# A fused attention and expert kernel: when the attention stage asks for its loads

## The chip, the cores and the metric

The kernel runs on one core of a Trainium2 chip. The core has a matrix engine (TensorE, PE in the profile; its weight loads are the row PEld), a vector engine (VectorE, DVE), a scalar engine (ScalarE, ACT), a general engine (GpSimd, POOL) and an engine that here only issues transfers (SyncE, SP). Each engine works through its own queue in order; the queues wait for each other through semaphores. Transfers between device memory and the on-chip memory run on 16 DMA engines. They are issued by SP (loads) and by POOL (results, and gathers and scatters by index).

The metric is the device time of the whole program in microseconds, the median of several runs. The kernel before took 645.92 us (three runs, 644.81 to 647.61).

## The reference: what is computed

Two blocks follow each other, on 8 sequences of 576 tokens with 8 heads of 64 values, all in float32.

```python
# attention, with a window of 64 tokens
scores = scale * np.matmul(q, k.transpose(0, 1, 3, 2))
mask = (rel >= 0) & (rel < window)            # rel = query position - key position
attn = softmax(np.where(mask, scores, -1e9))
x = np.matmul(attn, v)                        # then heads side by side: 512 values a token
...
# one expert of 8 for each token
logits = x @ w_gate                           # 512 x 8
local_gate = sigmoid(x @ w_local)
e = argmax(logits) if first token of a sequence or local_gate < 0.5 else e of the token before
p = softmax(logits)
h = np.maximum(x @ w1[e], 0.0)                # 512 x 1024
out = p[e] * (h @ w2[e])                      # 1024 x 512
```

The expert of a token depends on its attention output, so the sorting of tokens by expert (the router) stands between the two blocks.

## The kernel before, in words

**Attention** treats the 4608 tokens as 9 superchunks of 512, and the 8 heads as 4 pairs. A unit is one superchunk and one pair, written (sc, hp); there are 36, in the order (0, 0), (0, 1) and so on to (8, 3). For a unit TensorE multiplies keys with queries (`scores`, line 385), ScalarE takes the exponential (line 416), VectorE applies the mask (line 421; for some units a bias matmul at line 400 does it instead), TensorE multiplies with the values (`values`, line 431), and VectorE takes the reciprocals of the sums into `allr` (line 436) and scales the result into `x` (line 441). Scores run two units ahead of values. So the reciprocals at line 436, one for each unit and in order, are a clock by which units can be followed in the trace.

**What is loaded for a superchunk.** `kq` holds keys and queries, 2 MB, in a tile of the ring `ring` (four buffers of 2 MB, shared with the experts' weights). `va` holds the values, 1.0 MB, or 1.2 MB for the superchunks 4 to 8, which have extra room for gate columns; it has three buffers. From `va`, POOL and ScalarE copy a version shifted by 64 tokens, `vb` (lines 360 to 367). For the superchunks 4 to 8 there is also `vtt`, the turned values, 1 MB and one buffer, from which TensorE computes the gate logits of the values (`gates`, line 317). `gates(sc + 1)` runs in unit (sc, 2), and the shift to `vb` of superchunk sc + 1 begins in unit (sc, 0). At the end of a superchunk POOL writes `x`, 1 MB, to device memory (line 533).

**When it is loaded.** All these loads are issued by SP, in the order of the program. Superchunk 0 is asked for at the start. The loads of superchunk 1 stand behind a small transfer `until` (line 239), which reads one number of the first mask and so can't start before the mask is there; everything after it in SP's queue waits with it. The loads of superchunk 2 stand in the same way behind the reciprocals of unit (0, 0). The rest (sc + 2, for sc from 1 to 6) is placed in units (sc, 0) and (sc, 2): the whole of `va`, then two halves of `kq`, and in (sc, 2) the turned values. These wait for nothing but a free buffer: the buffer of `va` is free when the values of superchunk sc - 1 are done (line 228 in SP's waits), that of the turned values when `gates(sc + 1)` are done (line 223).

**The router** for the first part of the tokens runs beside attention (`rt.first`, in pieces handed out by `step`), mostly on VectorE; its table needs lines 790 to 975. It ends with writing each token's weight `ptw` to device memory (`weigh`, line 893, on SP) and with the table of rows for the first expert blocks.

**The experts** work in blocks of 256 tokens of one expert. A block's rows are gathered by index (POOL, line 1148), turned (line 1181), and multiplied with `w1` (line 1379 for the first blocks) and `w2` (line 1411). The first block is job -1. Its weights are asked for while attention still runs: `w1` in four pieces of 512 KB behind the reciprocals of (6, 3), `w2` likewise behind those of (7, 1), both at line 1167. Later blocks ask for their weights when a buffer of the ring is free.

**Order of work.** In attention the order on PE, ACT and SP is the program's own (`manual_schedule`, line 204). On VectorE and POOL a planner at build time orders the instructions, by its own costs and by when it thinks that their inputs are ready.

Of the kernel before, what the change touches and what calls it, by code (L numbers as in the profile page):

```python
# [8 lines left out]
F32 = mybir.dt.float32  # L9
# [6 lines left out]
ET = mybir.EngineType  # L16
# [3 lines left out]
P = 128  # L20
B, H, S, DH = 8, 8, 576, 64
D = H * DH
E, F = 8, 1024
DK, FK = D // P, F // P
# [19 lines left out]
PARTS = 4  # L44
# [16 lines left out]
SC = 4 * P  # L61
NSC = N // SC
HP = H // 2
# [3 lines left out]
VX = DH + 1  # L67
VW = VX + E + 1
GATED = range(4, NSC)
BIASED = [(4, 3), (5, 1), (5, 3), (6, 0), (6, 1), (6, 2), (6, 3)]  # L70
HALF = 0.8
STEP = 3.5
# [5 lines left out]
def row_of(t):  # L78

    return t + (t >= ZR)  # L80
# [87 lines left out]
def attention(ctx, tc, ring, kq, v3, v4, vt, vh, xs, lt, ok, wg, wg2, ident, rt, ex):  # L168
# [37 lines left out]
    kqs, qts, kts, vts, vas, vbs = {}, {}, {}, {}, {}, {}  # L206

    def width(sc):
        return VW if sc in GATED else VX

    def space(name, sc):
        return kp.tile([P, 4, H, width(sc)], F32, name=name, bufs=2 if name == "vb" else 3)


    vhs = tp.tile([P, HP, SC], F32, name="vtt")[:, :, :WIN]
# [2 lines left out]

    def load(sc, parts):
        for part in parts:  # L220
            if part == "turned":
                vts[sc] = tp.tile([P, HP, SC], F32, name="vtt")
                nc.sync.dma_start(out=vts[sc], in_=vt[GATED.index(sc)])
            elif isinstance(part, tuple):
                if sc not in vas:
                    vas[sc] = space("va", sc)
                src, h = v4[GATED.index(sc)] if sc in GATED else v3[sc], slice(*part)
                nc.sync.dma_start(out=vas[sc][:, :, h], in_=src[:, :, h])
            else:
                if sc not in kqs:  # L230
                    kqs[sc] = ring.tile([P, HP, 2, SC], F32, name="w")
                    kts[sc], qts[sc] = kqs[sc][:, :, 0], kqs[sc][:, :, 1]
                nc.sync.dma_start(out=kqs[sc][:, part], in_=kq[sc, :, part])

    late = cp.tile([1, 4], F32, name="late")

    def until(i, x):

        nc.sync.dma_start(out=late[:, i:i + 1], in_=x)

    pairs = slice(0, HP // 2), slice(HP // 2, HP)
    whole = (0, H)
    load(0, [slice(0, 1), slice(1, 2), (0, H // 2), pairs[1], (H // 2, H)])

    def warm(n):

        r = bank()
        for _ in range(n):
            nc.tensor.transpose(r[:, :P], ident, ident)
# [18 lines left out]
    masks = []  # L268
# [26 lines left out]
    allr = cp.tile([P, NSC, HP, 2, 4], F32, name="allr")  # L295
# [12 lines left out]
    def gates(sc):  # L308
# [115 lines left out]
    def values(sc, hp, p, x, g):  # L424
# [12 lines left out]
        rr = r.rearrange("p j (c o) -> p j c o", o=1)  # L437
        if sc in GATED:
            nc.vector.tensor_tensor(g[:, :, hp].rearrange("p c j e -> p j c e"), o[:, :, :, VX:],
# [1 line left out]
        nc.vector.tensor_tensor(x[:, :, hp].rearrange("p c j d -> p j c d"), o[:, :, :, :DH],  # L441
                                rr.to_broadcast([P, 2, 4, DH]), op=Alu.mult)

    units = [(sc, hp) for sc in range(NSC) for hp in range(HP)]
    ps = {}
    masked = []
    for u in units[:LEAD]:
# [2 lines left out]
    with tc.issue_after(masked[-1].ins):  # L450
        build_mask(1)
    warm(24)
    until(0, masks[0][:1, :1])
    load(1, [pairs[0], whole, pairs[1]])
    moves, gated, turned, old = (), None, None, None
    side = None
# [14 lines left out]
    for i, (sc, hp) in enumerate(units):  # L471
        if hp == 0:
            x, g = wk.tile([P, 4, HP, 2, DH], F32, name="x"), None
            if sc in GATED:
                g = wk.tile([P, 4, HP, 2, E + 1], F32, name="g")

        if 1 < i < len(units) - LEAD:
            ps[units[i + LEAD]] = scores(*units[i + LEAD])
        if hp == (0 if sc else 3) and sc + 1 < NSC:
            moves = shift(sc + 1)  # L480
        for _ in range(2 if sc else 4):
            next(moves, None) if moves else None

        if hp == 3 and sc + 1 in GATED:
            spread(sc + 1, gated)
        elif (sc, hp) == (1, 3):
            gates_ahead()
        elif (sc, hp) == (2, 3):
            back_ahead()
        if hp == 3 and sc not in GATED:  # L490
            turn(sc, x, 0)
            old = x
        elif sc and sc - 1 not in GATED:
            if hp == 0:
                turn(sc - 1, old, 1)
            elif hp == 2:
                logits(sc - 1, turned)

        if side is None and 4 * sc >= C1 and hp >= 2:
            side = rt.first(bank)  # L500
        step(not (hp == 3 and sc + 1 in GATED))
        values(sc, hp, ps.pop((sc, hp)), x, g)
        if i < 2:
            ps[units[i + LEAD]] = scores(*units[i + LEAD])
        if i == 0:
            shift_first(1)
            until(1, allr[:1, 0, 0, 0, :1])
            load(2, [pairs[0], whole, pairs[1]])
            nc.sync.dma_start(out=vhs, in_=vh)
        if i == 2 * HP:  # L510
            with tc.issue_after(masked[-1].ins):
                rt.prepare()
                build_bias()
        if hp == 1 and sc and sc - 1 not in GATED:
            turned = gates(sc - 1)
        if hp == 2 and sc + 1 in GATED:
            gated = gates(sc + 1)
        if 0 < sc < NSC - 2 and hp in (0, 2):
            load(sc + 2, [pairs[1]] if hp else [whole, pairs[0]])
        if hp == 2 and sc + 2 in GATED:  # L520
            load(sc + 2, ["turned"])
        if (sc, hp) == (NSC - 3, 3):
            ex.jobs = [ex.weights({}, -1, ("w1",), lambda: until(2, allr[:1, sc, hp, 0, :1]))]
            if side == ():
                ex.rows(ex.jobs[0], -1)
        step(not (hp == 2 and sc + 1 in GATED))
        if (sc, hp) == (NSC - 2, 1):
            ex.weights(ex.jobs[0], -1, ("w2",), lambda: until(3, allr[:1, sc, hp, 0, :1]))
        if hp == HP - 1:
            if sc in GATED:  # L530
                nc.vector.tensor_reduce(lt[:, 4 * sc:4 * sc + 4, :], g.rearrange("p c h j e -> p c e (h j)"),
                                        axis=AX.X, op=Alu.add)
            nc.gpsimd.dma_start(out=xs[row_of(sc * SC):row_of(sc * SC) + SC, :D].rearrange("(c p) d -> p c d", p=P),
                                in_=x.rearrange("p c h j d -> p c (h j d)"))
# [583 lines left out]
class Experts:  # L1118
# [33 lines left out]
        st["pw"] = [x[:, D:D + 1] for x in st["x"]]  # L1152
        return st

    def weights(self, st, n, names=("w1", "w2"), behind=lambda: None):
        ej, at = (self.tabs["ej1"], -1 - n) if n < 0 else (self.tabs["ej"], n)
        e = self.nc.values_load(ej[0:1, at:at + 1], engines=[ET.SP], min_val=0, max_val=E - 1,
                                skip_runtime_bounds_check_because="a count of experts, at most E - 1")
        behind()
        for name, w, a, b in (("w1", self.w1, DK, F), ("w2", self.w2, FK, D)):  # L1160
            if name not in names:
                continue
            t = self.ring.tile([P, a * b], F32, name="w")
            src = w[bass.ds(e, 1)].rearrange("o p x -> (o p) x")
            m = a * b // (PARTS if n < 0 else 1)
            for c in range(0, a * b, m):
                self.nc.sync.dma_start(out=t[:, c:c + m], in_=src[:, c:c + m])
            st[name] = t.rearrange("p (a b) -> p a b", a=a)
        return st

    def begin(self):
        self.jobs = [self.fetch(-1)]
# [395 lines left out]
```

## Time and profile before

| what | value |
|---|---|
| median of three runs | 645.92 us |
| the profiled execution's own time | 646.97 us |
| its span, first to last instruction | 645.2 us |
| mean granted TensorE clock | 0.997 |
| attention, about 0 to 136 us: TensorE busy | 119.42 of 136.00 us |
| experts, 136 to 632 us: TensorE busy | 493.76 of 496.00 us |
| the tail, 632 to 645.2 us: TensorE busy | 6.33 of 13.20 us |
| DMA in attention: share of the 16 engines, rate | 0.94, 356 GB/s |
| DMA in the experts' stage | 0.65, 237 GB/s |
| reciprocals of (0, 0), (2, 0), (6, 0), (7, 0) | 14.22, 41.94, 104.49, 115.13 us |
| reciprocals of (6, 3), (7, 3), (8, 2), (8, 3) | 111.90, 124.10, 131.62, 133.85 us |
| superchunk 8 asked for: `va`, turned values | 97.00, 108.59 us |
| its `gates` on TensorE, its shift on POOL | 118.54; 111.56 and 112.96 us |
| first matmul of the first expert block (w1, w2) | 133.7, 149.2 us |

All times in the trace count from the first instruction. Slices and windows give an engine's busy time; a matmul's end is modelled, so a busy TensorE need not be at its peak. "A <- B: t, n, m" in a list of waits means that A stood idle for B, t us in total, n times, m at the longest. "Issue" as the releaser means that the profile shows nothing that the engine waited for. A line of a timeline gives the start, the length, the engine, the line of the program, the operation and what it writes and reads.

### The profile page before, as it was taken

How to read it: one execution, taken by the hardware profiler on the slowest of the kernel's cores; microseconds unless marked ns; L12 is line 12 of the kernel's file. 1: busy time of each engine (PE TensorE's matmuls, PEld its weight loads, DVE VectorE, ACT ScalarE, POOL GpSimd, SP SyncE). 2: the span in 40 equal slices, each digit the busy share in tenths (PEclk: the TensorE clock that was granted, in tenths of full speed). 3: DMA queues.
4: the chain of work that ended last, by engine and by line, in shares of the span. 5: the costliest groups of instructions: out<-in, count | busy, mean ns of one | idle time of the engine just before them, and what ended most of it. 6: DMA issues, size and time to landing. Idle time of an engine off the chain costs nothing. (4 is left out here: it accounts for less than half of the span.)

```text
span 645.2 us, 14856 instructions
## 1 busy us (share of the span) xinstructions
PE 619.5 (96%) x6319; PEld 535.8 (83%) x6319; DVE 386.7 (60%) x730; ACT 199.9 (31%) x364; POOL 130.0 (20%) x132
## 2 busy tenths in 40 slices
PE   8889998899999999999999999999999999999995
PEld 7777776785859999978998999887997998899995
DVE  6676588853874865273553683362917752876730
ACT  4766665611473122112120312021211221122120
POOL 5322112320003202111212220221312022101101
PEclk9999999999999999999999999999999999999998
DMA  8999999969736655686957655769768557945501
GB/s 331 416 349 344 379 359 368 344 241 356 210 146 233 242 199 197 209 314 244 398 193 274 229 226 217 259 232 366 258 244 302 186 196 255 354 157 221 216 17 38
DMA packets 29318, 166.43 MB, mean 258 GB/s; under 512 B 8451, under 2 KB 9497, under 8 KB 20026
## 3 DMA queue, kind: packets, MB, share of 16 engines
q1 hardware_dynamic: 20394, 135.54, 57.8%
q0 software_dynamic: 8848, 29.85, 11.9%
q8 instruction: 52, 0.85, 0.5%
q14 instruction: 24, 0.20, 0.1%
HBM read 146.18 MB, written 19.59 MB: 257 GB/s over the span
## 5 line engine op out<-in xcount | busy, mean ns | idle before, releaser
L1361 POOL DMA_INDIRECT out_dram<-y,idx x36 | 41.3, 1148 | 347.3 <-DVE y L1297 169.6
L1240 PE MATMUL hp<-xs,ws 128*128 128x128 f32 x672 | 79.6, 275 | 0.0
L1288 PE MATMUL hp<-ws,hs 128*128 128x256 f32 x336 | 77.6, 380 | 0.0
L1240 PEld LDWEIGHTS hp<-xs,ws 128*128 128x128 f32 x672 | 77.3, 192 | 0.0
L1288 PEld LDWEIGHTS hp<-ws,hs 128*128 128x128 f32 x336 | 63.5, 190 | 9.3 <-issue 0.8
L1379 PE MATMUL hp<-xt,w 128*64 128x64 f32 (+2 forms) x640 | 66.3, 276 | 1.0 <-issue 1.0
L1379 PEld LDWEIGHTS hp<-xt,w 128*128 128x128 f32 (+1 forms) x640 | 61.2, 170 | 5.9 <-issue 2.5
L1297 DVE SCALAR_TENSOR_TENSOR y<-hp,xg,kept 128x256 f32<-128x256 f32 x42 | 19.7, 481 | 71.4 <-issue 47.0
L1251 DVE TENSOR_TENSOR h<-hp,keep 128x512 f32<-128x512 f32 x42 | 28.6, 690 | 53.0 <-PE hp L1240 53.0
L1148 POOL DMA_INDIRECT xg<-xs,gx x40 | 48.2, 1205 | 44.3 <-issue 37.6
L1411 PE MATMUL yp<-w,h 128*128 128x512 f32 x128 | 56.6, 593 | 0.0
L1240 PEld LDWEIGHTS hp<-xt,w 128*128 128x128 f32 x448 | 53.2, 192 | 2.7 <-issue 1.3
L1240 PE MATMUL hp<-xt,w 128*128 128x128 f32 x448 | 54.7, 275 | 0.0
L1288 PE MATMUL hp<-w,h 128*128 128x256 f32 x224 | 53.6, 382 | 0.0
L431 PE MATMUL xo<-vb,p 128*64 128x74 f32 (+1 forms) x576 | 44.2, 228 | 6.8 <-issue 3.7
L416 ACT ACTIVATE p<-sp 128x512 f32<-128x512 f32 x72 | 39.2, 596 | 37.1 <-PE sp L385 33.9
L385 PEld LDWEIGHTS sp<-w 64*64 64x64 f32 x1296 | 37.9, 134 | 13.1 <-issue 9.7
L421 DVE TENSOR_TENSOR p<-p,mask 128x1024 f32<-128x1024 f32 x29 | 36.5, 1258 | 19.2 <-ACT p L416 18.9
L431 PEld LDWEIGHTS xo<-vb,p 128*64 128x64 f32 x576 | 38.4, 137 | 10.0 <-issue 5.2
L385 PE MATMUL sp<-w 64*64 64x128 f32 (+1 forms) x1296 | 43.3, 265 | 3.3 <-issue 2.4
L1288 PEld LDWEIGHTS hp<-w,h 128*128 128x128 f32 x224 | 41.3, 190 | 5.6 <-issue 0.4
L431 PE MATMUL xo<-va,p 128*64 128x74 f32 (+1 forms) x576 | 44.5, 228 | 1.5 <-issue 1.5
(280 smaller groups left out, 934.0 us busy)
## 6 DMA issues: line engine op xcount, KB each, us to landing
w<-in_w_dram SPq DMA_DIRECT2D x42, 2048.0 KB, 8.7
w<-in_kq_dram SPq DMA_DIRECT2D x17, 1024.0 KB, 10.2
w<-in_w_dram SPq DMA_DIRECT2D x24, 512.0 KB, 10.0
xs<-x POOLq DMA_DIRECT2D x9, 1024.0 KB
va<-in_v_dram SPq DMA_DIRECT2D x5, 1184.0 KB
vtt<-in_vt_dram SPq DMA_DIRECT2D x5, 1024.0 KB
va<-in_v_dram SPq DMA_DIRECT2D x3, 1040.0 KB, 10.2
va<-in_v_dram SPq DMA_DIRECT2D x2, 520.0 KB, 7.0
```

Of the source, the lines that this page charges most:

```text
L385: nc.tensor.matmul(sp[j][c * WIN:(c + 1) * WIN, a:b], lhsT=kt[h, hp, block * WIN:(block + 1) * WIN], rhs=qt[h, hp, a:b], start=not biased, ...
L416: nc.scalar.activation(p[:, j], sp[j], Act.Exp, scale=DH ** -0.5)
L421: masked.append(nc.vector.tensor_tensor(p, p, m.to_broadcast([P, 2, SC]), op=Alu.mult))
L431: nc.tensor.matmul(xo[par * WIN:(par + 1) * WIN, j, s * VW:s * VW + n], lhsT=p[:, j, b * WIN:(b + 1) * WIN], rhs=w[:, s, 2 * hp + j, :n], ...
L1148: self.nc.gpsimd.indirect_dma_start(out=x, out_offset=None, in_=self.xs[:rows, :], in_offset=bass.IndirectOffsetOnAxis(ap=gx[:, s:s + 1], ...
L1240: nc.tensor.matmul(out[:, m, :], lhsT=a[:, kk, m * P:(m + 1) * P], rhs=b[:, kk, :], start=start and m + kk == 0, stop=stop and (m, kk) == ...
L1251: nc.vector.tensor_tensor(o, x, y, op=add)
L1288: nc.tensor.matmul(out, lhsT=a[:, m, :], rhs=b[:, m, :], start=start and m == 0, stop=stop and m == FK // 2 - 1, skip_group_check=True)
L1297: nc.vector.scalar_tensor_tensor(y[i][:, j * w:(j + 1) * w], x, pw[i], y2, Alu.mult, Alu.add)
L1361: self.nc.gpsimd.indirect_dma_start(out=self.out[:, :], out_offset=bass.IndirectOffsetOnAxis(ap=st["idx"][:, s:s + 1], axis=0), in_=y, in_ ...
L1379: nc.tensor.matmul(hp[a, i, :], lhsT=st["w1"][:, kk, m * P:(m + 1) * P][:, a], rhs=st["xt"][:, kk, :n], start=(kk == 0), stop=(kk == DK - 1))
L1411: nc.tensor.matmul(yp, lhsT=st["h"][:, m, i * P:(i + 1) * P], rhs=st["w2"][:, m, :], start=(m == 0), stop=(m == FK - 1))
```

## The change

The loads of the superchunks 2 to 8 are cut into four shares, one for each unit (sc, hp) of the superchunk two before. Each share stands in SP's queue behind `until` on that unit's reciprocals. The shares for hp = 0 and 1 hold half of `va` (two of its four chunks of 128 tokens) and one pair's part of `kq` (512 KB); those for hp = 2 and 3 hold half of the turned values (512 KB, superchunks 4 to 8 only) and one pair's part of `kq`. The first block's `w1` goes out in four pieces behind the units of superchunk 7, its `w2` in four behind those of superchunk 8, the last one without a wait. The number of the first block's expert is read by SP in unit (7, 0) instead of (6, 3). The loads of superchunks 0 and 1 stay. The loading of later blocks' weights is rewritten through the new function `piece` and issues what it did.

```diff
+UNITS = [(sc, hp) for sc in range(NSC) for hp in range(HP)]
+TURNED = "turned0", "turned1"
...
         for part in parts:
-            if part == "turned":
-                vts[sc] = tp.tile([P, HP, SC], F32, name="vtt")
-                nc.sync.dma_start(out=vts[sc], in_=vt[GATED.index(sc)])
+            if part in TURNED:
+                if sc not in vts:
+                    vts[sc] = tp.tile([P, HP, SC], F32, name="vtt")
+                h = pairs[TURNED.index(part)]
+                nc.sync.dma_start(out=vts[sc][:, h], in_=vt[GATED.index(sc), :, h])
+            elif isinstance(part, int):
+                if sc not in vas:
+                    vas[sc] = space("va", sc)
+                src, c = v4[GATED.index(sc)] if sc in GATED else v3[sc], slice(part, part + 2)
+                nc.sync.dma_start(out=vas[sc][:, c], in_=src[:, c])
...
-    late = cp.tile([1, 4], F32, name="late")
+    late = cp.tile([1, len(UNITS) + 1], F32, name="late")
...
+    def behind(sc, hp):
+        until(allr[:1, sc, hp, 0, :1])
...
         if i == 0:
             shift_first(1)
-            until(1, allr[:1, 0, 0, 0, :1])
-            load(2, [pairs[0], whole, pairs[1]])
-            nc.sync.dma_start(out=vhs, in_=vh)
...
-        if 0 < sc < NSC - 2 and hp in (0, 2):
-            load(sc + 2, [pairs[1]] if hp else [whole, pairs[0]])
-        if hp == 2 and sc + 2 in GATED:
-            load(sc + 2, ["turned"])
-        if (sc, hp) == (NSC - 3, 3):
-            ex.jobs = [ex.weights({}, -1, ("w1",), lambda: until(2, allr[:1, sc, hp, 0, :1]))]
-            if side == ():
-                ex.rows(ex.jobs[0], -1)
+        if sc < NSC - 2:
+            behind(sc, hp)
+            load(sc + 2, [*([2 * hp] if hp < 2 else TURNED[hp - 2:hp - 1] if sc + 2 in GATED else []), slice(hp, hp + 1)])
+        if i == 0:
+            nc.sync.dma_start(out=vhs, in_=vh)
+        if sc == NSC - 2:
+            behind(sc, hp)
+            if hp == 0:
+                ex.jobs = [ex.weights({}, -1, ())]
+                if side == ():
+                    ex.rows(ex.jobs[0], -1)
+            ex.piece(ex.jobs[0], "w1", hp)
         step(not (hp == 2 and sc + 1 in GATED))
-        if (sc, hp) == (NSC - 2, 1):
-            ex.weights(ex.jobs[0], -1, ("w2",), lambda: until(3, allr[:1, sc, hp, 0, :1]))
+        if sc == NSC - 1:
+            if hp < HP - 1:
+                behind(sc, hp)
+            ex.piece(ex.jobs[0], "w2", hp)
...
+    def piece(self, st, name, i):
+
+        a, b = (DK, F) if name == "w1" else (FK, D)
+        if name not in st:
+            st[name] = self.ring.tile([P, a * b], F32, name="w").rearrange("p (a b) -> p a b", a=a)
+        m = a * b // st["parts"]
+        src = (self.w1 if name == "w1" else self.w2)[bass.ds(st["e"], 1)].rearrange("o p x -> (o p) x")
+        self.nc.sync.dma_start(out=st[name].rearrange("p a b -> p (a b)")[:, i * m:(i + 1) * m],
+                               in_=src[:, i * m:(i + 1) * m])
```

More of the change, by code (lines that the diff above doesn't have):

```diff
@@ L233, in load, with until @@
                 nc.sync.dma_start(out=kqs[sc][:, part], in_=kq[sc, :, part])
-    late = cp.tile([1, 4], F32, name="late")
-    def until(i, x):
+    late = cp.tile([1, len(UNITS) + 1], F32, name="late")
+    def until(x):
+        i = next(held)
         nc.sync.dma_start(out=late[:, i:i + 1], in_=x)
+    def behind(sc, hp):
+        until(allr[:1, sc, hp, 0, :1])
+    held = iter(range(len(UNITS) + 1))
     pairs = slice(0, HP // 2), slice(HP // 2, HP)
@@ L442, in values @@
                                 rr.to_broadcast([P, 2, 4, DH]), op=Alu.mult)
-    units = [(sc, hp) for sc in range(NSC) for hp in range(HP)]
+    units = UNITS
     ps = {}
@@ L452, in attention @@
     warm(24)
-    until(0, masks[0][:1, :1])
+    until(masks[0][:1, :1])
     load(1, [pairs[0], whole, pairs[1]])
@@ L1153, in rows, with weights @@
         return st
-    def weights(self, st, n, names=("w1", "w2"), behind=lambda: None):
+    def weights(self, st, n, names=("w1", "w2")):
         ej, at = (self.tabs["ej1"], -1 - n) if n < 0 else (self.tabs["ej"], n)
[L1157 to L1168, printed above, removed]
-        return st
+        st["e"] = self.nc.values_load(ej[0:1, at:at + 1], engines=[ET.SP], min_val=0, max_val=E - 1,
+                                      skip_runtime_bounds_check_because="a count of experts, at most E - 1")
+        st["parts"] = PARTS if n < 0 else 1
+        for name in names:
+            for i in range(st["parts"]):
+                self.piece(st, name, i)
+        return st
+    def piece(self, st, name, i):
[6 more added lines that the diff above has]
+                               in_=src[:, i * m:(i + 1) * m])
     def begin(self):
```

## The prediction

> **What bounds the kernel now.** I read the page first: the span is TensorE's, 96% busy, and the chain that ended last shows only the tail, so time can only be won or lost where TensorE stands idle, or is made to.
>
> ```profile
> PE 619.5 (96%) x6319; PEld 535.8 (83%) x6319; DVE 386.7 (60%) x730; ACT 199.9 (31%) x364; POOL 130.0 (20%) x132
> ...
> q8 instruction: 52, 0.85, 0.5%
> ```
>
> (Queue q8: packets, MB, share.) The waits of TensorE say where. Read the first column as who waited, the right side as total, times, longest. Nearly all of it is "issue", time in which the profile shows nothing that was waited for. The rows left out wait for ScalarE (1.5, 0.8 and 0.6 us) or VectorE (0.9), or belong to the expert stage.
>
> ```profile
> PE xo L431 <- issue: 5.2, 6, 1.8
> PE r L249 <- POOL ident masks.py:199: 2.6, 1, 2.6
> PE sp L385 <- issue: 2.4, 4, 1.1
> PE xo L431 <- DVE x L441: 1.6, 2, 1.2
> ...
> PE xo L302 <- issue: 0.5, 1, 0.5
> ```
>
> These 8.1 us (5.2 + 2.4 + 0.5) are eleven gaps, all in attention. TensorE's timeline puts them at 20.48 (0.51), 27.33 (0.42), 33.53 (0.65), 39.51 (1.09), 46.08 (0.24), 51.91 (0.28), 76.00 (0.69), 100.10 (1.02), 106.59 (0.27), 123.25 (1.18) and 129.43 (1.75 us). Cutting the trace into windows from one gap to the next gives the cause away: look at the counts in brackets behind PE and PEld.
>
> ```profile
> 20.48:27.33 6.85, 5.86 (x127) 4.99 (x127) 4.89 (x8) 6.75 (x10) 2.30 (x3) 1.00 1.02 411
> 27.33:33.53 6.20, 5.55 (x129) 4.20 (x129) 3.24 (x5) 3.88 (x7) 1.69 (x2) 1.00 1.02 422
> 33.53:39.51 5.98, 4.89 (x126) 4.29 (x127) 3.31 (x6) 2.80 (x5) 1.91 (x2) 1.00 0.76 280
> 39.51:46.08 6.57, 6.15 (x129) 4.57 (x128) 5.37 (x26) 4.91 (x8) 1.75 (x4) 1.00 1.00 373
> ...
> 123.25:129.43 6.18, 4.42 (x128) 4.03 (x127) 5.32 (x10) 2.59 (x6) 0.81 (x1) 1.00 1.03 388
> ```
>
> Between gaps lie 253 to 258 instructions each time. The instruction queue moved 0.85 MB in 52 packets, 16.3 KB each; TensorE's 12638 instructions divided by 256 are 49. So I read a gap as TensorE waiting for its next block of instructions, which travels on the same DMA engines as the loads. The last two columns are the DMA share and GB/s: with 411 to 422 GB/s moving the engines are full. From 111 to 115 us they moved 250 GB/s, and TensorE worked 4.00 of 4.00 us through 251 instructions.
>
> That DMA is full as a whole matters too: 373 GB/s from 8 to 112 us against the 420 or so of its fullest windows. The queue's own waits show what paces the requests now: free buffers.
>
> ```profile
> SPq L228 <- PE xo L431: 40.7, 6, 13.5
> ...
> SPq L223 <- PE r L317: 30.1, 4, 8.5
> ...
> SPq L239 <- DVE allr L436: 5.7, 2, 5.3
> ```
>
> **The change, part by part.** Durations are of the profiled execution (646.97 us, span 645.2), which is 1.05 us above the median of 645.92; I carry differences over to the median.
>
> *Waits and requests on SP.* Waits by a 4-byte transfer go from 4 to 36 (mask 1, superchunks 0 to 6: 28, superchunk 7: 4, superchunk 8: 3). The three on allr took 0.62 to 0.66 us of the queue, so 32 more are 20.5 us at 0.64. Loads of superchunks 2 to 8 go from 26 to 52 requests of 0.33 to 0.46 us, another 10 us. A unit's share then costs SP about 0.64 + 2 x 0.4 = 1.4 us of the 3.4 us that a unit lasts. Nothing else is in the queue but the routing weights (109.0 us), so this is free while units last over 1.5 us.
>
> *What the new waits hold up.* Each waits for a unit's reciprocals. Behind it stand that unit's loads, and between units (6, 2) and (6, 3) the writes of ptw. Those already stand behind the turned load, issued at 108.59 once gates(7) were done; the new order reaches them at about 109 as well. POOL's queue keeps its order. The expert's number, read now after (7, 0) at 115.13, was computed by 96.3: nobody waits.
>
> *The gaps.* Superchunks 2 and 3 have no turned load, so the new requests of superchunks 0 and 1 (14.22 to 41.94 us by the reciprocals, 13.9 us each) are 3 MB of loads plus 1 MB of results, about 300 GB/s for 420. The gaps at 27.33, 33.53 and 39.51 (2.16 us) should shrink; bounds are 0 and 2.16, and I take 70%, 1.5, by the unhindered block at 111 to 115. From there to 115.13 us a superchunk moves 5.2 MB (kq 2, va 1.2, turned 1, results 1) per 14.6 us either way, 88% of 420 GB/s in decimal bytes; of the gaps at 46.08, 51.91 and 76.00 (1.21 us) I take 40%, 0.5. The two at 100.10 and 106.59 lie where VectorE is late anyway (below): 0. The gap at 20.48 keeps superchunk 1's burst: 0. At the end, w1 and w2 were asked for as 2 MB each at 114.64 and 121.56; now 0.5 MB a unit. Of 1.18 I take 30%, since the last superchunk's loads are still under way, of 1.75 60%: 1.4. Sum 3.4 us, with bounds 0 and 2.16 + 1.21 + 2.93 = 6.3. A loss is not excluded, since gaps move with the blocks' ends.
>
> [...]
>
> *Smaller requests.* The 0.5 MB pieces of w landed in 10.0 us (median), the 2 MB ones in 8.7; 1 MB of kq in 10.2. Size alone shows no cost here; I take 0.
>
> [...] The windows above hold 422 GB/s with requests of 1 to 1.2 MB in flight, and the sum stays with them.
>
> *Requests that come later.* Before, superchunk 8's va and kq went out at 97.00 us, and its turned values at 108.59. The new requests hang on VectorE, which does the router's table work in the middle of (5, 3):
>
> ```profile
> 93.32 0.20 DVE L436 RECIPROCAL allr<-xo 128x8 f32<-128x8 f32 x1
> ...
> 100.55 1.49 DVE L951 TENSOR_TENSOR rowh<-io,lo 128x1280 bf16<-128x1280 f32 x1
> 101.95 0.20 DVE L436 RECIPROCAL allr<-xo 128x8 f32<-128x8 f32 x1
> ...
> 111.90 0.20 DVE L436 RECIPROCAL allr<-xo 128x8 f32<-128x8 f32 x1
> ```
>
> So from 94 to 102 us nothing is asked for, and the queue runs dry. Then within 102 to 108 come 1 MB for superchunk 7, 1 MB of results and 3.2 MB for superchunk 8: 5.2 MB x 2.62 us (at 400 GB/s) from 103.6 is 117.2; ptw's small packets (the 112 to 114 window moved only 262 GB/s) put it near 120. Behind that comes the second half of superchunk 8's turned values, released at 111.90, issued after ptw near 113.6, landing at about 121.4. The matmuls of gates(8) run at 118.54, so TensorE stops for 2.9 us. The lower end is 0, if it lands in 3.8 us (the fastest row on the ring's tile); the upper, with the slowest, 14.4, is 114 + 14.4 - 119 = 9.4. I take 0.8, nearer the low end, because all of this moves with the router's place on VectorE, and a late TensorE there meets other waits.
>
> *The last quarter of w1* is released by (7, 3) at 124.10 and issued at about 125.0. The first expert matmul starts at 133.7. At the median of 10.0 it lands at 135.0 and costs about 0.5 us; at 3.8 it costs nothing, at 14.4 it costs 4.9. I take 0.3. w2's last piece goes out at about 132.5 and is needed at 149.2: 0. The halves of va are asked for at least 7 us before their copies (105.59 against 112.96 for superchunk 8), and POOL may be late there: 0.
>
> Sum: -3.4 + 0.8 + 0.3 = -2.3. The profiled execution would have taken 644.7, the median is 643.6 us.
>
> **Rivals.** *All gaps close and nothing is late* (14%): -6.3, 639.6 us. For it: light windows have no gap. Against: DMA stays 88% full in the middle.
>
> *The blocks come no sooner* (15%): mean DMA load is the same, the fetch has its own queue, and the lateness is hidden: 645.6 us. For it: the gaps at 46.08 and 51.91 were small with DMA at full 422 GB/s. Against: 111 to 115.
>
> *Slower: a late turned half* (20%): one mechanism, in superchunk 7, gates(8). With the 11.3 us that 1 MB of kq took to land between 90 and 136 us, the half lands at 114 + 11.3 = 125.3, 6.2 us after its matmuls. With half the gain, 1.7, that is +4.5: 650.4 us. It decides from the point where the lateness is over the gain plus 3.2 us. For it: the dry stretch of 94 to 102 us. Against: the half is 0.5 MB and slips as soon as the router moves.
>
> **How the numbers follow.** The forecast has 51%; its own range is 641 to 645.5, from the gain's bounds. About 3.2 us (0.5%) is what a measurement of this kernel can tell from no change. The forecast's 51% split into 24% beyond that and 27% within; with the first rival faster is 38%, with the second same is 42%, slower 20%. The range goes from 639.6 (all gaps closed) to 649.0, which leaves out the worse half of the slower rival.
>
> **What would show it.** Right: the issue gaps every 256 instructions after 24 us are under 0.4 us, DMA share in 24 to 40 us falls below 0.9, SP waits mostly on allr. Wrong: gaps of the same size; TensorE idle before L317 or the first L1379 on a load; VectorE's router work in another place.

## The result, and the profile after

The kernel with the change takes 650.55 us (median of 20 runs, 645.01 to 654.49), the kernel before 646.20 us (20 runs, 644.65 to 650.37) on the same chip. The ratio is 1.006, with a 95% interval of 1.0036 to 1.0084: slower by 0.6%, where I had forecast 0.4% faster. The value lies beyond the top of my range (649.0) and beside the price of my own slower rival (650.4). The profiled execution of the changed kernel took 652.41 us, span 650.7; that of the kernel before 646.97, span 645.2. The profiles are compared with each other below, so there are 5.4 us to explain in them, 1.1 us more than between the medians (4.35).

The page of the kernel after, the same two lines as shown before:

```profile
PE 623.3 (96%) x6319; PEld 537.1 (83%) x6319; DVE 387.7 (60%) x730; ACT 199.8 (31%) x364; POOL 131.3 (20%) x132
...
q8 instruction: 52, 0.85, 0.5%
```

TensorE's work is the same 6319 matmuls and the same 52 packets of instructions, but it is busy for 3.8 us more, and 1.7 us more of the span is idle. The mean granted clock is 0.987 for 0.997, and the same matmuls take longer: those from `vb` into `xo` 234 ns on average for 228. I had not looked for that.

The waits of TensorE in the kernel after (total, times, longest):

```profile
PE r L331 <- DMA vtt<-in_vt_dram: 4.1, 1, 4.1
PE xo L445 <- issue: 2.7, 2, 2.3
PE r L263 <- POOL ident masks.py:199: 2.6, 1, 2.6
PE xo L445 <- DVE x L455: 2.3, 2, 1.9
...
PE sp L399 <- ACT vb L381: 1.2, 1, 1.2
PE sp L399 <- issue: 0.8, 2, 0.4
...
PE xo L316 <- issue: 0.3, 1, 0.3
```

The issue waits fell from 8.1 to 3.8 us (2.7 + 0.8 + 0.3), and one of those left, 2.35 us at 57.76, is new. At the top stands a wait that the kernel before did not have: 4.1 us of `gates` (L331) for the turned values.

SP's timeline around that wait shows how it comes about (start, length, engine, line, what is written and read):

```profile
94.35 0.59 SPq L249 DMA_DIRECT2D late<-allr  x1
95.03 0.33 SPq L227 DMA_DIRECT2D vtt<-in_vt_dram  x1
95.42 0.45 SPq L242 DMA_DIRECT2D w<-in_kq_dram  x1
102.99 0.58 SPq L249 DMA_DIRECT2D late<-allr  x1
...
106.28 0.33 SPq L232 DMA_DIRECT2D va<-in_v_dram  x1
106.66 0.77 SPq L242 DMA_DIRECT2D w<-in_kq_dram  x1
107.53 0.59 SPq L249 DMA_DIRECT2D late<-allr  x1
108.16 0.39 SPq L232 DMA_DIRECT2D va<-in_v_dram  x1
108.60 0.53 SPq L242 DMA_DIRECT2D w<-in_kq_dram  x1
109.56 0.59 SPq L249 DMA_DIRECT2D late<-allr  x1
110.46 0.33 SPq L227 DMA_DIRECT2D vtt<-in_vt_dram  x1
111.05 0.82 SPq L242 DMA_DIRECT2D w<-in_kq_dram  x1
114.91 3.85 SPq L910 DMA_DIRECT2D xs<-ptw  x2
118.86 0.59 SPq L249 DMA_DIRECT2D late<-allr  x1
119.49 0.39 SPq L227 DMA_DIRECT2D vtt<-in_vt_dram  x1
```

Two things are to be read here. First, nothing is asked for from 95.9 to 103.0 us: `until` waits for the reciprocals of (5, 3), and these stand on VectorE behind the router's table and come at 102.76. Second, SP is ready for the writes of `ptw` at 111.87 and issues them at 114.91. SP's waits name what it stood for:

```profile
SPq L249 <- DVE allr L450: 28.4, 16, 4.5
SPq L249 <- DVE g L453: 24.1, 7, 7.3
...
SPq L910 <- DMA va<-in_v_dram: 3.0, 1, 3.0
```

`ptw` has nothing to do with `va`. In this trace SP's 169 transfers name eight completion semaphores (the marks by which a landing is told) in turn, and of the 161 after the first eight none goes out before the one eight places ahead of it has landed; six go out within 0.02 us of that landing. Count back in the timeline: eight requests before `ptw` stands the `va` half of 106.28. It lands at 114.89, and `ptw` goes out at 114.91. Before the change eight requests were some 8 MB; now every third is a 4-byte `until`, and the others are half as large. So `ptw` waits 3.0 us, its 1728 rows of 64 bytes (two transfers, 104 and 4 KB) take SP another 3.85 us, as they took 3.86 before, and the turned half behind them goes out at 119.49, though it was released by the reciprocals at 113.33. It lands when `gates(8)` can go on, at 126.67:

```profile
126.67 1.92 PE L331 MATMUL r<-vtt,wg2s 128*32 128x512 f32 x4 [4.12 <-DMA vtt<-in_vt_dram]
```

The last bracket is the idle time before the first matmul and what ended it.

The windows of the kernel after (stretch; us; busy time and count of PE, PEld, DVE, ACT, POOL; granted clock; DMA share; GB/s) show an early stretch, the dry queue, and then the clock:

```profile
27.30:37.88 10.58, 10.22 (x254) 8.41 (x255) 6.46 (x10) 6.25 (x12) 1.73 (x2) 1.00 0.92 316
...
58.00:60.00 2.00, 2.00 (x33) 1.56 (x34) 0.37 (x2) 0.00 (x0) 0.00 (x0) 0.50 1.03 424
...
102.00:104.00 2.00, 0.12 (x3) 0.12 (x5) 2.00 (x6) 1.77 (x3) 0.00 (x0) 1.00 0.00 0
104.00:106.00 2.00, 2.00 (x54) 1.92 (x58) 2.00 (x10) 0.00 (x0) 0.75 (x1) 0.79 0.78 113
106.00:108.00 2.00, 2.00 (x40) 1.88 (x34) 1.41 (x4) 0.93 (x2) 0.00 (x0) 0.50 0.80 186
...
124.00:126.00 2.00, 0.00 (x0) 0.00 (x0) 0.00 (x0) 0.00 (x0) 1.70 (x2) 0.91 1.03 418
126.00:128.00 2.00, 1.32 (x4) 0.18 (x4) 0.00 (x0) 0.00 (x0) 0.22 (x1) 0.50 1.01 381
128.00:130.00 2.00, 2.00 (x32) 1.48 (x34) 0.00 (x0) 0.59 (x1) 0.00 (x0) 0.50 0.97 354
```

In the first line 509 instructions pass without a gap, at 316 GB/s; in the windows of before it was 253 to 258 from one gap to the next. From 102 to 104 us nothing moves at all. During or shortly after three idle stretches the granted clock falls to half: 57.4 to 60.8, 105.2 to 108.6 and 125.7 to 132.5 us. In the profiled execution of the kernel before it is full throughout attention.

I then took the start of the same matmul in both traces, after minus before, and noted where the difference steps:

| place in the trace (time of before) | step, us |
|---|---|
| gaps at 33.53, 39.51 and 46.08, together | -2.25 |
| new issue gap before 57.76 of after | +2.39 |
| half clock behind it | +1.38 |
| gap at 76.00 | -1.05 |
| half clock, 105.2 to 108.6 of after | +0.68 |
| scores wait for ScalarE's copy of the second half of `va`, 119.28 of after | +1.67 |
| `gates(8)` wait for the turned half | +0.44, +4.28 |
| half clock, 125.7 to 132.5 of after | +2.88 |
| gaps at 123.25 and 129.43 | -1.40, -1.94 |
| small steps between these places, together | +0.42 |
| a stall at 547 in the trace of before, absent from that of after | -1.60 |

The steps add up to +5.9 for +5.5 of span. The stall at 547 is not of the change: four of the kernels below have it in their traces too, the others don't. The gain is there, 6.6 us of old gaps gone, and about 13.7 us of new loss stands against it: 4.7 for the turned half, 4.9 at half clock (0.4 of it a wait for ScalarE), 2.4 a new gap, 1.7 the `va` half.

How much of it is clock differs from one execution to the next. The mean granted clock of the changed kernel's 20 executions lies between 0.987 and 0.998, with a median of 0.992, and the profiled one, at 0.987, is at the low end. The six executions at 0.987 to 0.989 took 652.0 to 654.5 us, the seven at 0.994 and more 645.0 to 650.3. So the table shows more half clock than the median execution has.

### The profile page after: what moved, and what is told of

The parts are those of the page before. It is cut to its first block, busy times and chain, and to the rows that moved or that the text cites. A ratio compares the mean times of both kernels' runs of the same rounds, so it can differ in the third digit from the quotient of the medians.

```text
span 650.7 us, 14955 instructions
## 1 busy us (share of the span) xinstructions
PE 623.3 (96%) x6319; PEld 537.1 (83%) x6319; DVE 387.7 (60%) x730; ACT 199.8 (31%) x364; POOL 131.3 (20%) x132
## 5 line engine op out<-in xcount | busy, mean ns | idle before, releaser
L445 PEld LDWEIGHTS xo<-vb,p 128*64 128x64 f32 x576 | 40.1, 142 | 11.8 <-issue 6.0
L445 PE MATMUL xo<-vb,p 128*64 128x74 f32 (+1 forms) x576 | 45.6, 234 | 4.3 <-DVE x L455 2.3
L445 PE MATMUL xo<-va,p 128*64 128x74 f32 (+1 forms) x576 | 45.7, 234 | 2.3 <-issue 2.3
```

What stands on the lines that cost most here:

```text
L445: nc.tensor.matmul(xo[par * WIN:(par + 1) * WIN, j, s * VW:s * VW + n], lhsT=p[:, j, b * WIN:(b + 1) * WIN], rhs=w[:, s, 2 * hp + j, :n], ...
```

## The experiments

My theory after the result: the loss is in superchunks 7 and 8, whose requests come late, first for the router on VectorE and then for a full SP queue; the gain at the gaps is real. Rivals: the smaller requests cost by themselves; the lateness of the turned half alone explains it, without the queue; the gaps have nothing to do with the transfers. In the headings, "change" is the changed kernel and "before" the kernel before. Ratios are to the kernel before on the same chip, with 95% intervals; the kernel before took 646.2 to 648.7 us on the chips used, so the times expected are best read by the ratios.

### Change, the turned values asked for whole in (sc, 2)

```diff
-            load(sc + 2, [*([2 * hp] if hp < 2 else TURNED[hp - 2:hp - 1] if sc + 2 in GATED else []), slice(hp, hp + 1)])
+            load(sc + 2, [*([2 * hp] if hp < 2 else TURNED if hp == 2 and sc + 2 in GATED else []), slice(hp, hp + 1)])
```

> The change, but both halves of the turned values go out in unit (sc, 2), the second no longer behind the reciprocals of (sc, 3). Theory (superchunk 8's loads come too late, after VectorE's router block): TensorE's wait of 4.1 us before gates(8) and the half clock after it (about 2.7 us) go, some 7 us less than the change: 643 to 645 us. Rival (waits and small requests cost by themselves, anywhere in attention): within 2 us of the change, 649 to 651.

Measured: 647.55 us, ratio 1.0021 (0.9989 to 1.0053). The wait of `gates` is gone, but `ptw` keeps SP for 7.40 us from 112.53 on, and the rows of the first expert block, which are gathered after it, are late. SP's line and the waits of TensorE in this kernel:

```profile
112.53 7.40 SPq L910 DMA_DIRECT2D xs<-ptw  x2
```

```profile
PE xo L445 <- issue: 3.6, 4, 1.1
PE xo L445 <- DVE x L455: 2.8, 2, 2.5
...
PE tp L1202 <- DMA xg<-xs,gx: 2.2, 2, 1.4
```

POOL issues the first gather at 125.43 here, at 118.36 in the kernel before. What follows: the turned half was worth about 0.4%, less than I expected, since what is behind it in the queue is late next. The clock is at half twice, from 103.4 to 106.8 after a wait of 2.5 us for VectorE's `x`, and from 134.1 to 137.5 behind the late rows.

### Change, the writes of `ptw` behind the next unit's loads

```diff
-        self.weigh(0)
+        self.later = [lambda: self.weigh(0)]
...
+        while rt.later:
+            rt.later.pop()()
         if sc == NSC - 2:
             behind(sc, hp)
```

> The change, with the router's ptw writes moved in SP's queue from before to behind the loads of unit (6, 3). Theory (late loads, and ptw's writes in front of the turned half as the larger part of it): the half goes out near 114 instead of 119.5 us and lands about 120 to 121, the wait before gates(8) falls to under 1 us, 644 to 646 us. If the full queue alone is the cause: the half still lands at 123 or later, a wait of 2 us or more, 648 to 650. Rival (waits and small requests cost anywhere): 650.

Measured: 653.71 us, 1.0116 (1.0083 to 1.0150). The turned half goes out at 113.62 and `gates(8)` wait only 0.15 us. But `ptw` goes out from 115.07 to 121.2, the gathers follow at 126.71 and 128.84, and the waits of TensorE in this kernel are led by

```profile
PE tp L1206 <- DMA xg<-xs,gx: 5.8, 2, 3.2
```

with the clock at half from 135.9 to 142.7. A miss: the order of these two in a queue that is too full only chooses which of them is late, and the gathers are the dearer ones.

### Change, the first `ptw` writes issued by POOL

```diff
-                self.nc.sync.dma_start(
+                (self.nc.sync if part else self.nc.gpsimd).dma_start(
                     out=xs[row_of(a):row_of(a) + b - a, D:].rearrange("(c p) o -> p c o", p=p),
```

> The change, with the router's first ptw writes issued by POOL instead of SP. Theory (in SP's queue these writes hold up the turned half, and the full queue with its eight semaphores holds up the writes and so the gathered rows): the half goes out near 114 us, the writes near 105 to 110; the waits before gates(8) and for gathered rows together fall under 2 us: 645 to 648 us. Rival (the full queue alone makes superchunk 8 late): gates(8) still waits 2 us or more, 649 to 651.

Measured: 647.88 us, 1.0024 (1.0000 to 1.0048). SP's timeline in this kernel, around the same place:

```profile
112.16 0.59 SPq L249 DMA_DIRECT2D late<-allr  x1
113.37 0.33 SPq L227 DMA_DIRECT2D vtt<-in_vt_dram  x1
```

The turned half goes out 6.1 us earlier than in the changed kernel, the gathers at 117.04 and 118.50; neither is waited for, and the clock stays full in attention. So what SP does between the reciprocals of (6, 3) and the turned half, `ptw` and its wait, makes the half late. Whether a loss remains is not clear: the interval begins at 1.0000, and the profiled execution (646.82) is no slower than that of the kernel before. TensorE's waits in it hold issue gaps (4.5 us at L445), the copy of `va` (1.4) and a piece of `kq` (0.9).

### Before, with the second turned half behind (6, 3)

```diff
+                h = pairs[0] if sc == NSC - 1 else slice(HP)
-                nc.sync.dma_start(out=vts[sc], in_=vt[GATED.index(sc)])
+                nc.sync.dma_start(out=vts[sc][:, h], in_=vt[GATED.index(sc), :, h])
+            elif part == "rest":
+                nc.sync.dma_start(out=vts[sc][:, pairs[1]], in_=vt[GATED.index(sc), :, pairs[1]])
...
         if (sc, hp) == (NSC - 3, 3):
+            until(4, allr[:1, sc, hp, 0, :1])
+            load(NSC - 1, ["rest"])
```

> The kernel before, with one thing of the change: the second half of superchunk 8's turned values goes out behind the reciprocals of (6, 3). Theory (it is late because the queue is full with superchunk 8's other loads): here these are in by then, the half lands within 6 us of about 113.5, TensorE waits 0 to 1 us: 645.5 to 647.5 us. Rival (a request behind (6, 3) is too late by itself): a wait of 3 us or more and a half clock after it, 650 or more.

Measured: 646.94 us, 1.0008 (0.9988 to 1.0028).

```profile
113.53 0.38 SPq L226 DMA_DIRECT2D vtt<-in_vt_dram  x1
```

The half goes out just where my prediction had it, and nobody waits for it. The request behind (6, 3) is therefore not what costs; it costs when the queue is already behind. (The clock is at half once in this trace, from 103.7 to 107.1, after a wait of 2.5 us for VectorE's `x`, before this half is asked for.)

### Before, with the second turned half behind (7, 1)

The half is split off as in the last run; only its place is another.

```diff
+        if (sc, hp) == (NSC - 2, 1):
+            until(4, allr[:1, sc, hp, 0, :1])
+            load(NSC - 1, ["rest"])
```

> The kernel before, with the second half of superchunk 8's turned values held back further, behind the reciprocals of (7, 1) near 118 us, behind the loads of w1. It measures the price of this one lateness by itself. Theory (a TensorE idle for some 4 us pays the wait and then a half clock of 3.4 or 6.8 us): a wait of 3 to 7 us before gates(8) and 5 to 10 us more than the kernel before, more than the wait itself. Rival (the wait alone, made up in part later): 2 to 5 us more, no half clock.

Measured: 654.64 us, 1.0133 (1.0099 to 1.0167), of four executions. This puts the lateness of the change (here 119.08) into the kernel before, without its small requests. The wait and then the windows of this kernel:

```profile
PE r L320 <- DMA vtt<-in_vt_dram: 8.5, 1, 8.5
```

```profile
124.00:126.00 2.00, 0.00 (x0) 0.00 (x0) 0.00 (x0) 0.00 (x0) 0.00 (x0) 0.50 1.03 407
...
128.00:130.00 2.00, 2.00 (x10) 0.34 (x14) 0.00 (x0) 0.08 (x1) 0.00 (x0) 0.50 1.03 422
```

The wait is 8.5 us, longer than the 3 to 7 that I expected and twice that of the change: TensorE is at `gates(8)` 3 us earlier here, and the half, behind 2 MB of `w1`, lands 1.3 us later. By the starts of the same matmuls it loses 9.1 us at `gates(8)` and 2.9 more at half clock (123.6 to 133.8), and gets 3.3 back, because the gaps at 123.25 and 129.43 are gone in this trace, where TensorE is late, as in that of the change. A half asked for 5.5 us later than in the last run, which lost nothing, costs 8.3 us of time (654.64 against 646.31 of the kernel before).

### Change, without the waits for the reciprocals

```diff
-            behind(sc, hp)
+            if i == 0:
+                behind(sc, hp)
             load(sc + 2, [*([2 * hp] if hp < 2 else TURNED[hp - 2:hp - 1] if sc + 2 in GATED else []), slice(hp, hp + 1)])
```

> The change with its shares, but for superchunks 3 to 8 without the waits on reciprocals: a share goes out when its buffer is free. Theory (the waits make superchunk 8's loads late; the shares themselves cost nothing): no dry stretch near 102 us, no wait before gates(8), gathered rows in time: 644 to 646.5 us, the early instruction gaps about as before. Rival (twice as many requests, of half the size and on the same eight semaphores, are slow): the wait before gates(8) or the one for gathered rows stays, 648 or more.

Measured: 647.92 us, 0.9992 (0.9969 to 1.0016). The small shares are all there, and no time is lost: the rival of the small requests falls. The gain is gone too, with issue gaps of 6.7 us (6.2 + 0.5) for 8.1; the waits of TensorE in this kernel begin

```profile
PE xo L445 <- issue: 6.2, 7, 2.5
PE r L263 <- POOL ident masks.py:199: 2.6, 1, 2.6
...
PE sp L399 <- ACT vb L381: 0.8, 1, 0.8
```

No clock falls in attention, and the turned half is in time (asked for at 115.43). Both the gain at the gaps and the loss hang on the waits, as the theory says.

### Change, each share a unit earlier

```diff
-            behind(sc, hp)
+            behind(*units[max(i - 1, 0)])
```

> The change with each share of attention's loads behind the reciprocals of one unit earlier. Theory (they hang on VectorE's router block): the share of (5, 3) goes out near 95 instead of 102 us and nothing runs dry; superchunk 8's turned half goes out 2 to 5 us sooner, the wait before gates(8) falls from 4.1 to 0 to 2 us: 644 to 648 us. Rival (the end is crowded by the amount, not by the start): the wait stays over 3 us, 649 to 651.

Measured: 650.80 us, 1.0036 (1.0015 to 1.0057). That is above the 644 to 648 that I expected. The wait of `gates` goes and the clock stays full in attention, yet at most a part of the loss comes back: the ratio falls from 1.0060 to 1.0036, and the two intervals overlap. TensorE's waits hold more issue gaps (2.5 + 3.7 us against 2.7 + 0.8) and still 1.4 us for the `va` copy. A gap more or less is as large as what is to be gained here; why these gaps came back I did not settle.

### Superchunks 7 and 8 as before, the rest as changed

```diff
-        if sc < NSC - 2:
+        if sc < NSC - 4:
             behind(sc, hp)
             load(sc + 2, [*([2 * hp] if hp < 2 else TURNED[hp - 2:hp - 1] if sc + 2 in GATED else []), slice(hp, hp + 1)])
+        elif sc < NSC - 2:
+            if hp in (0, 2):
+                load(sc + 2, [pairs[1]] if hp else [whole, pairs[0]])
+            if hp == 2:
+                load(sc + 2, TURNED)
```

> The change for superchunks 2 to 6 and for the weights, but superchunks 7 and 8 asked for as before (whole, as buffers are free). Theory (gaps before 50 us shrink by some 2 us, those of the end by 2 to 3, and superchunk 8 is in time): 641.5 to 644 us, faster than both kernels. Rival (gaps and half clocks only move to other places): 646 to 648.

Measured: 647.22 us, 0.9976 (0.9953 to 0.9999). The window where the queue of the changed kernel ran dry reads in this one

```profile
100.00:103.00 3.00, 1.76 (x49) 1.46 (x49) 2.84 (x12) 2.03 (x3) 0.19 (x1) 1.00 1.03 422
```

and there is no wait for the turned values. From 1.006 to 0.9976 the last two superchunks are worth 0.8% (of two comparisons, on two chips). This is where the loss was. The gain of 0.24% is less than the 0.4% and more that I expected.

### Only superchunks 2 and 3 and the weights as changed

```diff
-        if sc < NSC - 2:
+        if sc < 2:
             behind(sc, hp)
...
+        elif sc < NSC - 2:
+            if hp in (0, 2):
+                load(sc + 2, [pairs[1]] if hp else [whole, pairs[0]])
+            if hp == 2:
+                load(sc + 2, TURNED)
```

> The change for superchunks 2 and 3 and for the weights; superchunks 4 to 8 asked for as before. Theory (the gain lies in the early gaps, about 2 us, and in those of the end, 1 to 3 us; everything between only moves gaps): 0.3 to 0.7% under the kernel before in the same rounds. Rival (no gain is left without the middle): within 0.2%.

Measured: 643.06 us, 0.9953 (0.9935 to 0.9971), against 646.31 us of the kernel before: faster than both kernels. TensorE's waits in it:

```profile
PE sp L399 <- issue: 2.6, 3, 1.9
PE xo L445 <- DVE x L455: 2.3, 2, 2.0
PE xo L445 <- issue: 1.9, 3, 1.3
```

The issue gaps are 4.7 us instead of 8.1 (0.2 of it in a row not shown), and nobody waits for a late request. The gain, 3.25 us between the medians, is of the size that the prediction had for the gaps (3.4 us), but the trace does not show that it comes from the early gaps: one of these, at 39.92, is 1.9 us here and 1.1 before, and behind it the clock is at half from 40.1 to 43.5. By the starts of the same matmuls this one execution has gained nothing by 76 us and 1.7 us by 140, most of it at the two gaps of the end; another 1.6 us is the stall at 547 of the other trace. Whether the middle superchunks add or take something is not told apart: the intervals of this run and the last overlap.

### Change, the weights as before

```diff
-            behind(sc, hp)
-            if hp == 0:
-                ex.jobs = [ex.weights({}, -1, ())]
...
+        if (sc, hp) == (NSC - 3, 3):
+            ex.jobs = [ex.weights({}, -1, ("w1",))]
...
+        if (sc, hp) == (NSC - 2, 1):
+            behind(sc, hp)
+            for part in range(PARTS):
+                ex.piece(ex.jobs[0], "w2", part)
```

> The change for attention's loads alone: w1 goes out as one block of four pieces in (6, 3), w2 likewise behind (7, 1). Theory (late loads of superchunk 8): the wait before gates(8) stays at 3 to 6 us, and the two instruction gaps of the end (1.2 and 1.8 us before) come back: 651 to 654 us. Rival (the weights' shares are what costs): 646 to 648.

Measured: 649.88 us, 1.0050 (1.0029 to 1.0071), with the wait of `gates` at 4.3 us. The loss is not in the weights. I had expected the gaps at 123.25 and 129.43 back, and 651 to 654 us; they stayed away (-1.0 and -2.0 by the matmuls' starts). So the weights' shares are not needed for that: a TensorE that stands at `gates(8)` is enough, as in the run with (7, 1), whose weights are also those of the kernel before.

### Before, the weights as changed

The edit is to the changed kernel; it gives attention's loads back their old places.

```diff
-            behind(sc, hp)
-            load(sc + 2, [*([2 * hp] if hp < 2 else TURNED[hp - 2:hp - 1] if sc + 2 in GATED else []), slice(hp, hp + 1)])
+            if i == 0:
+                behind(sc, hp)
+                load(2, [pairs[0], whole, pairs[1]])
+            elif sc and hp in (0, 2):
+                load(sc + 2, [pairs[1]] if hp else [whole, pairs[0]])
+            if hp == 2 and sc + 2 in GATED:
+                load(sc + 2, TURNED)
```

> The kernel before with the change's shares for w1 and w2 alone; attention's loads as before, the turned values in two requests at the same place. Theory (lighter DMA at the end closes the instruction gaps of 123.25 and 129.43 us, 2.9 us together): 643 to 645 us, if w1's last quarter is in time. Rival (gaps don't hang on DMA traffic): 646 to 647. If w1's last quarter is late: TensorE waits before the first expert block, 647 or more.

Measured: 646.92 us, 0.9988 (0.9970 to 1.0006): no difference that can be told, where I expected up to 2.9 us. In its trace nobody waits for `w1`, and the two gaps at the end, 1.18 and 1.75 us before, are 0.27 and 0.65, with no wait at `gates(8)` to hide them.

### Before, with less traffic

```diff
+                if sc > 1:
+                    kqs[sc], kts[sc], qts[sc] = kqs[1], kts[1], qts[1]
+                    continue
                 if sc not in kqs:
```

> The kernel before, leaving out the loads of keys and queries for superchunks 2 to 8: those of superchunk 1 are used again, so the numbers computed are others, while the instructions are nearly the same. It takes 2 MB of some 5 MB off each superchunk's transfers. Theory (a gap of TensorE every 256 instructions is its next block of instructions, late because the DMA engines are full): the gaps marked issue, 8.1 us before, fall under 2.5 us, attention ends 4 to 6 us sooner. Rival (gaps don't hang on DMA traffic): they stay at 6 to 8 us.

This kernel leaves out the loads of keys and queries from superchunk 2 on, so it computes other numbers with nearly the same instructions. Measured: 640.37 us (one execution), span 638.6. The window from 8 to 112 us, first of this kernel, then of the kernel before:

```profile
8.00:112.00 104.00, 94.69 (x2323) 78.50 (x2313) 79.58 (x199) 69.89 (x118) 29.11 (x36) 1.00 0.68 242
```

```profile
8.00:112.00 104.00, 93.47 (x2205) 76.35 (x2199) 75.58 (x192) 66.79 (x113) 26.83 (x34) 1.00 0.97 373
```

With 242 GB/s instead of 373, TensorE gets 118 matmuls further in the same time. Of the gaps between 24 and 112 us 0.56 us is left, of 4.66 before; those at the end, where `w1` and `w2` move as before, stay (0.92 and 1.76). All issue gaps of attention together are 3.9 us, not under 2.5 as I expected. In this run the gaps go with the traffic: the third rival falls.

## Why the prediction was wrong, step by step

- **What bounds the kernel, and the gaps.** Right as far as the runs go: with less traffic, 242 GB/s for 373, 0.56 us of 4.66 is left between 24 and 112 us (last run above). That what comes late is the next block of instructions was my reading of the counts. The traces' records of single DMA packets fit it: each of the eleven gaps of the kernel before ends 2.2 to 2.6 us after the start of a 16 KB packet on the instruction queue q8, and so do the five of the changed kernel; the new one of 57.76 follows a packet of 55.45. The size was too small for the old gaps: I took 3.4 us, and 6.6 went, a little over the upper bound of 6.3, though those of the end went in part because TensorE was late. Of the signs that I had named, the gaps left after 24 us are 0.42, 0.36 and 0.34 us beside the new one, but the DMA share from 24 to 40 us stayed at 0.92 (0.93 before); only the rate fell, from 365 to 328 GB/s. I had written that gaps move; one of 2.35 us moved in at 57.76. The two at the end shrink by the weights' shares alone, but go also without them when TensorE stands at `gates(8)`; in the changed kernel the two can't be told apart.
- **Waits and requests on SP, taken as free.** Wrong. I added up SP's own time (1.4 us of 3.4 a unit) and left out what a request of this program holds besides: a place among eight in flight (none of 161 transfers goes out before the one eight places ahead has landed). "The new order reaches them at about 109 as well" was 114.91, after 3.0 us for a `va` half.
- **Requests that come later, "I take 0.8".** This is the step that failed most. The dry stretch came as described, and so did the place, `gates(8)`. But I had the half issued at 113.6 and landing at 121.4; it was 119.49 and 126.7. TensorE waited 4.1 us, within my bounds of 0 to 9.4, and the term measured 4.7 for 0.8. The runs with `ptw` on POOL and with `ptw` behind, where the half goes out at 113.37 and 113.62 and is waited for not at all and for 0.15 us, show that my 113.6 would have cost almost nothing: it was the queue that I mis-sized, not the transfer (7.2 us, and 7.8 in my sum). I had even worked out 2.9 us and then taken 0.8 on the ground that a late TensorE meets other waits; the gaps at 123.25 and 129.43 did vanish, but the clock came on top.
- **The clock, no term at all.** 4.9 us by the matmuls' starts in the profiled execution, less in the median one. The profile of before shows full clock throughout attention, and I took that as given for a TensorE that is made to wait. This share is read from the traces and from the clocks of the 20 executions; no run took the clock away by itself.
- **Halves of `va`, "0".** 1.7 us: the second half was asked for at 108.16, POOL waited for it until 117.65, and the scores stood behind ScalarE's copy of it. I had named POOL as possibly late and costed it at nothing.
- **Smaller requests, 0.** Right: without the waits the same shares give 0.9992. With SP's requests in flight of 0.5 MB each the engines moved 418 GB/s from 124 to 126 us.
- **The last quarter of `w1`, 0.3, and `w2`, 0.** No wait for either is seen.
- **The slower rival.** It named the mechanism, the superchunk and the place, and its 650.4 is 0.15 us off the median. Its way there was different: 6.2 us of lateness and half the gain, where the runs show 4.7 us of lateness, a gain of 6.6 us, and 9.0 us of clock, `va` and a new gap, which it didn't have. The terms didn't agree; that the value did was luck.

Not settled: what keeps three repaired kernels (turned values whole, `ptw` on POOL, a unit earlier) at 1.002 to 1.004 instead of 0.995; the intervals of the first two reach down to 1. Their traces show the late copy of `va`, late rows, moved gaps and, in the first, half clock, each 1 to 2 us; no run parts them.

## What to carry to other kernels

Requests can be spread over the units: done for two superchunks and the weights it is worth 0.5% here (643.06 us for 646.31). But spread them only where the event that releases them can't be delayed by other work, so look at what else stands on the releasing engine (here a router on VectorE, in the last two superchunks). Count requests in flight on a queue, not only its issue time: in this program a 4-byte transfer used as a wait takes the same one of eight places as 1 MB, and `ptw` waited 3.0 us for a place. Price a new stall of a busy TensorE with the clock behind it, not with the wait alone: here 2.9 us followed a wait of 4.1.

## What the runs showed of the hardware

**The clock.** In the kernel after, the granted clock fell to half three times in attention, for 3.4, 3.4 and 6.8 us (57.4 to 60.8, 105.2 to 108.6 and 125.7 to 132.5). TensorE stood for 2.35 us up to 57.76, for 1.91 us up to 103.88, and for 4.12 us up to 126.67; the first two in its timeline:

```profile
57.76 0.27 PE L445 MATMUL xo<-va,p 128*64 128x65 f32 x1 [2.35 <-issue]
```

```profile
103.88 0.28 PE L445 MATMUL xo<-vb,p 128*64 128x74 f32 x1 [1.91 <-DVE x L455]
```

It does not follow every such pause: 1.75 us at 129.43 in the kernel before brought none, while 1.42 and 0.76 us, before matmuls 1.4 us apart in the run with the turned values whole, were followed by half clock from 134.1 to 137.5. It lasted 10.2 us in the run with (7, 1), beside a wait of 8.5. What decides whether a pause is followed by half clock, and for how long, the runs do not show.

**The gaps.** In the kernel before, 253 to 258 instructions lie between neighbouring gaps of the windows shown. At 16 gaps, in the kernel before and the changed one, TensorE stood for 0.24 to 2.35 us and went on 2.2 to 2.6 us after the start of a 16 KB packet of the instruction queue q8. With a third less traffic (242 GB/s for 373) 0.56 us of these waits was left between 24 and 112 us, of 4.66.

**The queue.** In the kernel after, SP never had more than eight transfers on their way, whether of 4 bytes or of 512 KB and more: each of the 161 after the first eight went out after the landing of the one eight places ahead. The writes of `ptw`, 108 KB in rows of 64 bytes, took SP 1.8 us (second half behind (7, 1)) to 7.4 us (turned values whole).
